# Weight-splitting steps dealt out singly between output pairs, and the softmax numerators normalised on GpSimd, in a fused attention and ELU-MLP kernel

## Chip, cores and metric

One core of one Trainium2 chip runs the whole program. The time is device microseconds of an execution; before the change the median of three runs is 647.06 us (645.84 to 647.61).

## What is computed

Four batches of 12 heads, 448 tokens, head size 64. Attention with a soft cap on the scores, then a two-layer MLP with an ELU between the layers:

```python
scores = cap * tanh(q @ k.T / sqrt(64) / cap)
attn = softmax(scores)                  # sum + 1e-9
x = (attn @ v)                          # (4, 12, 448, 64) -> (1792, 768)
h = x @ w_in                            # 768 -> 2048
g = where(h > 0, h, exp(min(h, 0)) - 1)
out = g @ w_out                         # 2048 -> 768
```

Inputs and output are float32. Each MLP product is done as three TensorE products of rounded halves (high by high, high by low, low by high).

## The kernel before

**Attention.** Twenty-four pairs of heads are worked in 12 rounds of two pairs. A table of times (`AT`, `END`) is sorted once, and that sorted list is the order of every engine's instructions; each engine then runs its own list in order. In a round TensorE makes scores (`tile0`, `scores`), ScalarE does the tanh and the exponential (`act`), TensorE multiplies with the values (`values`, line 408) and makes the row sums (`sums`). VectorE (DVE) adds exponentials (`add`, line 430), splits q and k into high and low halves (lines 358 and 361), copies numerators and sums out of PSUM (`take`, lines 445 and 448), adds and inverts the denominators (`invert`, lines 460 and 463) and also splits the weights and tokens of the MLP. The denominators go through DMAs on SyncE's queue: sums to `den` (line 453), the reciprocals to DRAM (line 465), and from there spread over the partitions into `rb` (`spread`, line 475), two DMAs for each pair. `normalise` (line 480) multiplies the numerator `num` of a pair by its `rb` and gives the tokens `x`. The numerator has five buffers, `rb` two.

**Weights.** There are 32 weight tiles of 128x768, four for each of the 8 rounds of the MLP: two of `w_in`, then two of `w_out`. A tile is split in five steps by a generator (`Weights.steps`): step 1 three DVE operations (lines 123 to 125), step 2 a scaled copy on ScalarE (line 135), step 3 a DVE operation (line 139) and an integer add on GpSimd (line 142), step 4 the rounded high half `wh` on ScalarE (line 149), step 5 the low half `wl` on DVE (line 153). The first four tiles are split in the attention part. There are six `wh` buffers, so tile k takes over that of tile k-6.

**MLP.** A unit is one round r and one block t of tokens (three blocks of 512 columns, one of 256). `Moe.run` deals the units out, software-pipelined by one: it issues `first` of unit i (two hidden tiles `h` and their ELU, ending in `gh` and `gl`), then `second` of unit i-1 (three output pairs e = 0, 2, 4 in a PSUM ring of three, each drained into `acc`: in round 0 by ScalarE, line 285, later by a DVE add, line 300). The weight steps stand around `second`: half of `WRUN[t]` ahead of it and half behind it, 20 steps a round. Steps and drains share ScalarE and DVE, each in program order.

Of the kernel before, what the change touches and what calls it, by code (L numbers as in the profile page):

```python
# [12 lines left out]
ALU = mybir.AluOpType  # L13
# [19 lines left out]
TINY = 2.0**-15  # L33
BLOCKS = [(t, min(BANK, B * S - t)) for t in range(0, B * S, BANK)]
NB = len(BLOCKS)
WRUN = (6, 6, 4, 4)


def pieces(b):

    out = []
    for t, (t0, n) in enumerate(BLOCKS):
        lo, hi = max(t0, b * S), min(t0 + n, (b + 1) * S)
        if lo < hi:
            out.append((t, lo - t0, lo - b * S, hi - lo))
    return out
# [31 lines left out]
class Weights:  # L78
# [77 lines left out]
    def run(self, n):  # L156

        for _ in range(n):
            if self.now is None:
                self.now = self.steps()  # L160
            if next(self.now, self) is self:
                self.now = None

    def get(self, f, second):
        return self.split[f // FT * 2 * FT + f % FT + FT * second]
# [48 lines left out]
class Moe:  # L214
# [54 lines left out]
            if i:  # L269
                self.elu(r, t, i, h)  # L270

    def second(self, r, t):
        nc = self.nc
        width = BLOCKS[t][1]
        end = (r, t) == (NR - 1, NB - 1)
        for e in range(0, NC, 2):
            if end and e == NC - 2:
                continue
            s = self.ps.tile([P, 2, BANK], F32, name=f"o{r}_{t}_{e}", tag="s", bufs=3)[:, :, :width]
            for k in range(2):  # L280
                self.outputs(s[:, k], r, t, e + k)
            if r == 0:
                o = self.late.tile([P, 2, width], F32, name=f"acc{t}_{e}", tag=f"acc{t}", bufs=NC // 2)
                self.acc[t, e] = o
                nc.scalar.activation(out=o, in_=s, func=AF.Copy)  # L285
            else:
                self.finish(r, t, e, 2, s, self.acc[t, e])
        if end:
            for k in range(2):
                s = self.ps.tile([P, 1, BANK], F32, name=f"last{k}", tag=f"pv{k}", bufs=1)[:, :, :width]  # L290
                self.outputs(s[:, 0], r, t, NC - 2 + k)
                self.finish(r, t, NC - 2 + k, 1, s, self.acc[t, NC - 2][:, k : k + 1])
# [13 lines left out]
    def run(self):  # L306

        units = [(r, t) for r in range(NR) for t in range(NB)]
        for i in range(1, len(units) + 1):
            if i < len(units):  # L310
                behind = ()
                if i + 1 < NB:
                    behind = [(b * PPB + c, i + 1) for c in range(PPB) for b in range(B)
                              if any(k == i + 1 for k, *_ in pieces(b))]
                self.first(*units[i], behind)
            n = WRUN[units[i - 1][1]]
            self.wt.run(n // 2)
            self.second(*units[i - 1])
            self.wt.run(n - n // 2)
            self.wt.ahead()  # L320


class Attention:
# [153 lines left out]

    def normalise(self, p):
        x = self.x.new(p)
        self.nc.vector.tensor_tensor(out=x, in0=self.num.pop(p), in1=self.rec.pop(p), op=ALU.mult)  # L480

    def run(self, weights, moe, raw, rawv):
        self.raw.update(enumerate(raw))
# [231 lines left out]
```

## Time and profile before

| what | value |
|---|---|
| median of the runs shown | 647.06 us |
| the profiled execution, its own time | 648.52 us |
| its span in the trace | 646.7 us |
| TensorE busy, share of the span | 97% |
| DVE, ScalarE, GpSimd busy | 72%, 46%, 9% |
| mean granted clock of TensorE | 0.996 |

Busy shares are of the whole span, which holds two stages: the attention up to about 177 us and the MLP behind it. TensorE's busy time is modelled, with ends of matmuls that overlap the next one, so a full TensorE is read from the starts of its matmuls rather than from the share.

### The profile page before, as it was taken

The page shows a single profiled execution, that of the slowest core. Times are in us where ns is not written, and L with a number is a line of the kernel's source. Part 1 is how long each engine was busy: PE and PEld are TensorE (multiplying, and loading weights), DVE is VectorE, ACT ScalarE, POOL GpSimd, SP SyncE. Part 2 cuts the span into 40 slices and gives each one's busy share as a digit, 9 for nine tenths or more (in the row PEclk, how much of TensorE's full clock was granted, in tenths as well). Part 3 has the DMA queues.
Part 4 walks back from the last instruction along what each step waited for, and adds up shares of the span by engine and source line. Part 5 has one row for each costly group of instructions (what it writes and reads, how often), then busy time and mean ns, then how long its engine had stood idle before and what let it go on. Part 6 is the DMA issues. An engine that isn't in the chain of part 4 may idle for free.

```text
span 646.7 us, 8796 instructions
## 1 busy us (share of the span) xinstructions
PE 629.4 (97%) x3408; PEld 463.0 (72%) x3408; DVE 463.8 (72%) x696; ACT 296.7 (46%) x396; POOL 61.2 (9%) x40
## 2 busy tenths in 40 slices
PE   5999999999999899999999999999999999999997
PEld 3334444334478788888888888888888888888886
DVE  4789999999667744776767577666857766776454
ACT  6999999999916544222231322223132322222110
POOL 0010100101001111121111111011111111211000
PEclk9999999999999999999999999999999999999999
DMA  4445565544123111121111111121111111200224
GB/s 162 140 141 186 158 185 148 168 125 132 32 77 126 51 49 50 49 98 31 68 50 50 49 50 55 43 76 71 50 50 50 50 50 49 70 30 0 98 97 152
DMA packets 30065, 54.38 MB, mean 84 GB/s; under 512 B 13377, under 2 KB 17473, under 8 KB 30017
## 3 DMA queue, kind: packets, MB, share of 16 engines
q1 hardware_dynamic: 30016, 53.75, 25.7%
q8 instruction: 29, 0.48, 0.3%
q14 instruction: 20, 0.16, 0.1%
HBM read 47.97 MB, written 5.59 MB: 83 GB/s over the span
## 4 chain that ended last, share of the span: by engine, by line
PE 78%; DVE 13%; DMA 3%; ACT 2%; issue 2%; POOL 1%; SPq 1%; DVEq 0%; POOLq 0%; ACTq 0%
PE o L226 11%; PE o L227 11%; PE o L228 11%; PE h L226 11%; PE h L227 11%; PE h L228 11%; PE pv L408 6%; PE s L366 4%; DVE u L430 3%; DVE xl L211 2%; PE sum L439 2%; DVE qkl L361 1%; DVE num L445 1%; PE s L383 1%; DMA den<-sums 1%
## 5 line engine op out<-in xcount | busy, mean ns | idle before, releaser
L226 PE MATMUL o<-gh,wh 128*128 128x512 f32 (+1 forms) x380 | 138.8, 365 | 2.7 <-ACT acc L285 2.7
L227 PE MATMUL o<-gl,wh 128*128 128x512 f32 (+1 forms) x380 | 138.9, 365 | 0.0
L228 PE MATMUL o<-gh,wl 128*128 128x512 f32 (+1 forms) x380 | 138.7, 365 | 0.0
L227 PE MATMUL h<-xl,wh 128*128 128x512 f32 x288 | 112.2, 390 | 0.3 <-DVE xl L211 0.3
L226 PE MATMUL h<-xh,wh 128*128 128x512 f32 x288 | 112.4, 390 | 0.0
L228 PE MATMUL h<-xh,wl 128*128 128x512 f32 x288 | 112.1, 389 | 0.0
L300 DVE TENSOR_TENSOR acc<-o,acc 128x1024 f32<-128x1024 f32 (+1 forms) x83 | 88.6, 1091 | 31.8 <-PE o L228 31.8
L240 ACT ACTIVATE e<-h 128x512 f32<-128x512 f32 (+1 forms) x64 | 34.7, 542 | 138.8 <-PE h L228 138.8
L401 ACT ACTIVATE p<-s,cap 128x896 f32<-128x896 f32 x84 | 84.7, 1008 | 2.7
L399 ACT ACTIVATE s<-s,tsc 128x896 f32<-128x896 f32 x84 | 81.9, 975 | 5.3 <-PE s L383 2.8
L226 PEld LDWEIGHTS o<-gh,wh 128*128 128x128 f32 x380 | 72.1, 190 | 14.5 <-ACT acc L285 2.9
L408 PE MATMUL pv<-p,vf 128*64 128x448 f32 x368 | 79.3, 552 | 3.0 <-DVE num L445 3.0
L228 PEld LDWEIGHTS o<-gh,wl 128*128 128x128 f32 x380 | 72.1, 190 | 11.4
L227 PEld LDWEIGHTS o<-gl,wh 128*128 128x128 f32 x380 | 72.0, 190 | 11.4
L249 ACT ACTIVATE gh<-e 128x512 fp32r<-128x512 f32 (+1 forms) x64 | 37.0, 578 | 90.2 <-DVE e L244 90.2
L250 DVE TENSOR_TENSOR gl<-e,gh 128x512 fp32r<-128x512 f32 (+1 forms) x64 | 40.0, 626 | 41.2 <-ACT gh L249 41.2
L142 POOL TENSOR_TENSOR pre<-pre,wq 128x768 int32<-128x768 int32 x18 | 34.7, 1929 | 339.7 <-DVE pre L139 339.7
L241 DVE TENSOR_SCALAR e<-e 128x512 f32<-128x512 f32 (+1 forms) x64 | 25.0, 391 | 56.5 <-ACT e L240 56.5
L226 PEld LDWEIGHTS h<-xh,wh 128*128 128x128 f32 x288 | 54.1, 188 | 12.4 <-DVE e L244 0.7
L227 PEld LDWEIGHTS h<-xl,wh 128*128 128x128 f32 x288 | 54.1, 188 | 11.6 <-DVE xl L211 0.7
L228 PEld LDWEIGHTS h<-xh,wl 128*128 128x128 f32 x288 | 54.1, 188 | 11.3
L408 PEld LDWEIGHTS pv<-p,vf 128*64 128x64 f32 x368 | 22.3, 136 | 44.1 <-issue 31.6
(78 smaller groups left out, 770.6 us busy)
## 6 DMA issues: line engine op xcount, KB each, us to landing
pre<-in_w_dram SPq DMA_DIRECT2D x18, 768.0 KB, 4.2
wr<-in_w_dram SPq DMA_DIRECT2D x14, 768.0 KB, 4.2
raw<-in_qk_dram SPq DMA_DIRECT2D x22, 448.0 KB, 4.5
vf<-in_v_dram SPq DMA_DIRECT2D x23, 256.0 KB, 4.1
rb<-rec SPq DMA_DIRECT2D x48, 112.0 KB, 2.9
out_dram<-acc SPq DMA_DIRECT2D x9, 512.0 KB, 2.7
den<-sums SPq DMA_DIRECT2D x96, 1.8 KB, 2.3
pre<-in_qk_dram SPq DMA_DIRECT2D x2, 256.0 KB, 4.1
```

Of the source, the lines that this page charges most:

```text
L142: nc.gpsimd.tensor_tensor(out=vi, in0=vi, in1=q, op=ALU.add)
L226: mm(acc, wh[:, m, :], ph, start=first, stop=False)
L227: mm(acc, wh[:, m, :], pl, start=False, stop=False)
L228: mm(acc, wl[:, m, :], ph, start=False, stop=last)
L240: nc.scalar.activation(out=ev, in_=h, func=AF.Exp)
L249: nc.scalar.activation(out=gh, in_=ev, func=AF.Copy)
L250: nc.vector.tensor_tensor(out=gl, in0=ev, in1=gh.bitcast(F32), op=ALU.subtract)
L300: self.nc.vector.tensor_tensor(out=o, in0=s, in1=o, op=ALU.add)
L366: yield lambda a=a, b=b, i=i: self.nc.tensor.matmul(s, a[o, k], b[o, :S], start=i == 0, stop=i == 2)
L399: self.nc.scalar.activation(out=s, in_=s, func=AF.Tanh, scale=self.con.tsc[:, 0:1])
L401: self.nc.scalar.activation(out=pt, in_=s, func=AF.Exp, scale=self.con.cap[:, 0:1])
L408: self.nc.tensor.matmul(out[o, :S], w[j], x[j], **flags)
```

## The change

```diff
-WRUN = (6, 6, 4, 4)
+WRUN = ((2, 2, 1, 1), (2, 2, 1, 1), (2, 1, 1, 1), (1, 1, 1, 1))
...
-    def second(self, r, t):
+    def second(self, r, t, steps=()):
...
                 self.finish(r, t, e, 2, s, self.acc[t, e])
+            self.wt.run(steps[e // 2])
...
-            n = WRUN[units[i - 1][1]]
-            self.wt.run(n // 2)
-            self.second(*units[i - 1])
-            self.wt.run(n - n // 2)
+            steps = WRUN[units[i - 1][1]]
+            self.wt.run(steps[0])
+            self.second(*units[i - 1], steps[1:])
             self.wt.ahead()
...
     def normalise(self, p):
         x = self.x.new(p)
-        self.nc.vector.tensor_tensor(out=x, in0=self.num.pop(p), in1=self.rec.pop(p), op=ALU.mult)
+        self.nc.gpsimd.tensor_tensor(out=x, in0=self.num.pop(p), in1=self.rec.pop(p), op=ALU.mult)
```

The first number of a tuple is the count of steps ahead of `second`, the other three stand behind the drain of each output pair. A round now has 6 + 6 + 5 + 4 = 21 steps where it had 20.

Three places show what this does to the order.

On GpSimd in the attention, ahead of the weight add of tile 1 and of tile 2 (`x` are the tokens of a pair, `wq` the copy of step 2 that the weight add reads):

```order
 L142 TENSOR_TENSOR pre_81<-pre_81,wq1_671 128x768
+L480 TENSOR_TENSOR x4_871<-num4_514,rb4_763 128x448
+L480 TENSOR_TENSOR x5_873<-num5_581,rb5_768 128x448
+L480 TENSOR_TENSOR x6_1027<-num6_667,rb6_917 128x448
+L480 TENSOR_TENSOR x7_1029<-num7_735,rb7_922 128x448
+L480 TENSOR_TENSOR x8_1185<-num8_821,rb8_1075 128x448
+L480 TENSOR_TENSOR x9_1187<-num9_887,rb9_1080 128x448
 L142 TENSOR_TENSOR pre_81<-pre_81,wq2_1120 128x768
```

The 24 multiplications have left DVE's list for GpSimd's, where they stand between the few weight adds and wait for nothing but their `rb` and what is ahead of them there.

On ScalarE in the MLP, behind the ELU of unit (0, 2), where output unit (0, 1) is drained:

```order
 L135 ACTIVATE wq5_2225<-wr5_2076 128x768
-L149 ACTIVATE wh5_2305<-wv5_2224 128x768
-L285 ACTIVATE acc1_0_2321<-o0_1_0_2308 128x1024
-L285 ACTIVATE acc1_2_2336<-o0_1_2_2323 128x1024
-L285 ACTIVATE acc1_4_2351<-o0_1_4_2338 128x1024
-L135 ACTIVATE wq6_2354<-pre_81 128x768
+L285 ACTIVATE acc1_0_2318<-o0_1_0_2305 128x1024
+L149 ACTIVATE wh5_2320<-wv5_2224 128x768
+L285 ACTIVATE acc1_2_2337<-o0_1_2_2324 128x1024
+L285 ACTIVATE acc1_4_2356<-o0_1_4_2343 128x1024
+L135 ACTIVATE wq6_2339<-pre_81 128x768
```

The drain of the first output pair now stands ahead of `wh5`, which waits for the weight add on GpSimd.

On DVE in round 6, behind the ELU of unit (6, 2), as it is now (before the change `wl30` stood one unit later, behind all drains of unit (6, 2)):

```order
L139 SCALAR_TENSOR_TENSOR pre_81<-pre_81 128x768
L301 TENSOR_TENSOR acc1_0_2318<-o6_1_0_4946,acc1_0_2318 128x1024
L153 TENSOR_TENSOR wl30_4944<-pre_81,wh30_4943 128x768
L123 SCALAR_TENSOR_TENSOR wv31_4961<-wr31_4885 128x768
L124 TENSOR_SCALAR wv31_4961<-wv31_4961 128x768
L125 TENSOR_SCALAR wv31_4961<-wv31_4961 128x768
L301 TENSOR_TENSOR acc1_2_2337<-o6_1_2_4966,acc1_2_2337 128x1024
L301 TENSOR_TENSOR acc1_4_2356<-o6_1_4_4981,acc1_4_2356 128x1024
```

With one step more in each round the splitting has come six steps ahead by round 6: the step that needs the buffer of the round's first weight tile stands ahead of the last unit that reads that tile, and two drains stand behind it.

## Rows read from the trace of the kernel before

**Rows 1.** Chain that ended last: start us, us, work; one round apart.
```profile
45.47 0.91 PE s L383 x8
...
59.01 0.91 PE s L383 x8
```

**Rows 2.** Busy time by stretch, us (instructions), then granted clock, DMA share, GB/s.
```profile
60.00:80.00 20.00, 20.00 (x138) 7.90 (x132) 19.52 (x30) 19.59 (x22) 2.60 (x1) 1.00 0.52 157
...
120.00:140.00 20.00, 19.22 (x134) 8.28 (x134) 19.83 (x37) 19.09 (x20) 0.00 (x0) 1.00 0.49 135
...
226.00:228.00 2.00, 2.00 (x6) 1.57 (x5) 0.94 (x3) 1.18 (x3) 0.00 (x0) 0.50 0.00 0
```

**Rows 3.** Timeline of DVE, attention: start us, us, engine, line, operation, [idle before].
```profile
104.67 0.23 DVE L460 SCALAR_TENSOR_TENSOR den<-den,eps 64x28 f32<-64x28 f32 x1
...
134.39 1.08 DVE L480 TENSOR_TENSOR x<-num,rb 128x448 f32<-128x448 f32 x2
...
148.30 0.23 DVE L460 SCALAR_TENSOR_TENSOR den<-den,eps 64x28 f32<-64x28 f32 x1
```

**Rows 4.** Timeline of GpSimd, the weight add of tile 1.
```profile
74.20 2.60 POOL L142 TENSOR_TENSOR pre<-pre,wq 128x768 int32<-128x768 int32 x1 [26.62 <-DVE pre L139]
```

**Rows 5.** Timeline of DVE beside that add.
```profile
74.04 1.09 DVE L430 TENSOR_TENSOR u<-p,p 128x896 f32<-128x896 f32 x1
75.04 0.62 DVE L448 COPY sums<-sum 128x448 f32<-128x448 f32 x1
75.58 2.18 DVE L430 TENSOR_TENSOR u<-u,p 128x896 f32<-128x896 f32 x1
```

**Rows 6.** Groups by line and shape, count | busy us, mean ns | idle before, releaser.
```profile
L142 POOL TENSOR_TENSOR wv<-wv,wq 128x768 int32<-128x768 int32 x14 | 25.8, 1846 | 188.0 <-DVE wv L139 188.0
...
L124 DVE TENSOR_SCALAR wv<-wv 128x768 f32<-128x768 f32 x14 | 7.8, 561 | 0.5
...
L300 DVE TENSOR_TENSOR acc<-o,acc 128x1024 f32<-128x1024 f32 x63 | 75.9, 1221 | 30.8 <-PE o L228 30.8
```

**Rows 7.** Timeline of SyncE's queue: the DMAs that spread reciprocals, last two rounds.
```profile
177.68 2.37 SPq L475 DMA_DIRECT2D rb<-rec  x4
...
189.04 2.37 SPq L475 DMA_DIRECT2D rb<-rec  x4
```

**Rows 8.** Timeline of DVE from the end of the attention.
```profile
181.23 4.10 DVE L211 TENSOR_TENSOR xl<-x,xh 128x384 fp32r<-128x384 f32 x12
...
192.49 0.62 DVE L480 TENSOR_TENSOR x<-num,rb 128x448 f32<-128x448 f32 x1 [3.18 <-DMA rb<-rec]
...
219.31 0.95 DVE L139 SCALAR_TENSOR_TENSOR wv<-wr,wv 128x768 int32<-128x768 int32 x1
```

**Rows 9.** Timeline of TensorE, 184 to 247 us.
```profile
184.38 0.50 PE L227 MATMUL h<-xl,wh 128*128 128x512 f32 x1 [0.27 <-DVE xl L211]
...
221.12 0.28 PE L228 MATMUL h<-xb,wl 128*128 128x256 f32 x1
...
224.14 0.50 PE L226 MATMUL o<-gh,wh 128*128 128x512 f32 x1 [2.75 <-ACT acc L285]
...
225.19 0.63 PE L227 MATMUL o<-gl,wh 128*128 128x512 f32 x1
...
228.59 0.39 PE L226 MATMUL o<-gh,wh 128*128 128x512 f32 x1
228.82 0.40 PE L227 MATMUL o<-gl,wh 128*128 128x512 f32 x1
...
234.04 0.39 PE L226 MATMUL h<-xh,wh 128*128 128x512 f32 x1
...
242.20 0.28 PE L226 MATMUL o<-gh,wh 128*128 128x256 f32 x1
...
246.52 0.40 PE L226 MATMUL h<-xh,wh 128*128 128x512 f32 x1
```

**Rows 10.** Timeline of ScalarE at the end of round 0's second unit.
```profile
222.33 0.84 ACT L149 ACTIVATE wh<-wv 128x768 fp32r<-128x768 f32 x1 [2.86 <-POOL wv L142]
223.08 2.83 ACT L285 ACTIVATE acc<-o 128x1024 f32<-128x1024 f32 x3
```

## The prediction, made before the changed kernel ran

> **What bounds the kernel now.** I read first the starts of TensorE's matmuls, then the chain that ended last, then the busy time by stretch, then each engine's timeline where two engines meet.
>
> In the MLP TensorE runs matmul behind matmul: 0.23 us from the start at 228.59 to that at 228.82 [rows 9], a wide half unit in 8.16 us (234.04 to 242.20), a narrow one in 4.32 us (242.20 to 246.52). No other engine's work counts there unless TensorE stops. It stops once: between 221.12 and 224.14 us, 2.75 us of it waiting for a drain on ScalarE [rows 9]. That drain stood behind `wh5`, which had waited 2.86 us for the weight add on GpSimd [rows 10], which had waited for the DVE operation at 219.31 [rows 8]. After the stop the granted clock is 0.50 from 226 to 228 us [rows 2], the 1.2 GHz level: the eight matmuls from 225.19 to 228.59 take 0.425 us each [rows 9] instead of 0.23, which is 1.6 us. The stop costs 2.75 + 1.6 = 4.3 us.
>
> In the attention the bound changes hands. Around 50 us the chain runs through TensorE, a round in 59.01 - 45.47 = 13.54 us [rows 1]. From about 90 to 148 us it runs through DVE: the inversions at 104.67 and 148.30 are three rounds apart [rows 3], 14.54 us each, and DVE is busy 19.83 of 20 us [rows 2]. Here a DVE microsecond is a program microsecond. Earlier, from 60 to 80 us, DVE has 0.48 us of slack in 20 [rows 2].
>
> **The normalising.** Two multiplications leave DVE in each round, 1.08 us together [rows 3]. If that were all, the four rounds bound by DVE would fall to TensorE's 13.54 us: -1.0 us each, -4.0 us.
>
> GpSimd's price is bounded by its nearest row, the weight add: 1.85 us for 768 columns [rows 6]. In proportion, 448 columns take 1.08 us; I take that as an estimate. GpSimd itself has time for it; the question is DVE. Two groups show the two engines shutting each other out [rows 4, 5]. The add was released at 74.20, while DVE ran an addition with two SBUF operands; it took 2.60 us, 0.75 longer than alone, so it began to work at about 74.95, when that addition had read its operands. DVE's next addition was dispatched at 75.58 and took 2.18 us instead of 1.09: it stood until the add was done at 76.80. The copy from PSUM at 75.04 ran beside the add at its usual length. So a multiplication on GpSimd stops DVE for up to 1.08 us, unless DVE just then copies from PSUM (four copies of about 0.54 us a round, lines 445 and 448).
>
> The Trainium skill says the same: SBUF — State Buffer, section "Who interferes with whom", has a DVE instruction with two SBUF inputs contend with a GpSimd instruction that reads SBUF, and the trace agrees (2.18 against 1.09 us).
>
> When does GpSimd start? In the last round the spreading DMAs are issued from 189.04 [rows 7] and DVE's wait for the first `rb` ends at 192.49 [rows 8]: 3.45 us behind the first issue, and the second pair's some 1.2 us later, by the spacing of the four issues. That is about six microseconds before DVE used to multiply, in the dense part of its round. What a multiplication costs DVE lies between 0 (inside copies), 0.54 (it starts with a copy and the next operation waits for the rest) and 1.08. The one handover in the rows came with a copy next in line, which speaks for the lower part; but GpSimd got in at 74.95, ahead of DVE's next start at 75.04, which speaks for the upper. I take 0.6. Ten multiplications (x8 to x17) fall into the dense stretch: 10 x (0.6 - 0.54) = **+0.6 us**, bounds -4.0 and 10 x (1.08 - 0.54) = +5.4. The others meet slack and are entered at nothing; without it each pair would cost up to 1.1 us.
>
> Behind them: a numerator copy now also waits for the multiplication five pairs earlier, which is done a round before; x10 stands behind the weight add of tile 2 on GpSimd and x14 behind that of tile 3, which only makes `x` later, and `x` is read rounds later.
>
> **The end of the attention.** x20 and x21 become ready at 177.68 + 3.45 = 181.1 and 182.3 us [rows 7]; DVE starts twelve `xl` subtractions, two SBUF operands each, at 181.23 [rows 8], and TensorE is already waiting 0.27 us for the seventh at 184.38 [rows 9]. The first multiplication stops them about 0.95 us; the second 1.08 or, if DVE goes on, nothing. **+1.4 us**, bounds 0 and +2.0. In return DVE drops the multiplications x20 to x23 and the 3.18 us wait in front of x22 [rows 8]. That work is the beginning of the lateness that ends in the stop at 221 us, so DVE comes there earlier relative to TensorE even after the two stops by x22 and x23.
>
> **Dealing the steps singly.** In round 0 ScalarE's drain of the first pair of unit (0, 1) comes ahead of `wh5`. With the old times it would start at about 219.5, behind `wq5`, and end a microsecond later, before TensorE asks at 221.4; the second pair's drain, behind `wh5`, would end at 224.2 for a TensorE that asks at 224.1. So the stop goes even without an earlier DVE: **-4.3 us**, bounds -4.5 and 0. The same swap at `wh4`, one unit earlier, delays a drain for which TensorE asks about three microseconds later.
>
> In the other rounds TensorE does not stop, so there is nothing to gain. There is something to lose: 21 steps a round. In round 6 `wh30` needs the buffer of tile 24, which is read until half of the narrow `first` is done. Counting from the start of the wide `first` of unit (6, 2): 8.16 + 8.16 + 2.16 = 18.5, then about 0.3 to be seen, 0.85 for `wh30`, 0.95 for `wl30`, as for line 139 [rows 8], 0.95 + 2 x 0.56 for lines 123 to 125, the 0.56 being line 124's [rows 6], and 1.22 for the drain [rows 6]: 23.9. TensorE asks for that tile at 16.32 + 4.32 + 2.72 = 23.4. **+0.5 us**, bounds 0 and 2.1 (with the lower clock behind it). In round 5 only `wl26` is in front, and the drain is done at 21.8: in time.
>
> **Sum.** +0.6 + 1.4 - 4.3 + 0.5 = -1.8 us. Against the profiled execution, 648.52 us, that is 646.7; its time is 1.46 us above the median of the runs, so for the median I say 647.06 - 1.8 = **645.3 us**.
>
> **Rivals.**
> 1. *GpSimd slips between DVE's operations for nearly nothing.* For it: the copy beside the add was not slowed [rows 5]. Against it: 2.18 us. Then -4.0 + 0 - 4.3 + 0.5 = -7.8: 639.3 us. Chance 0.15.
> 2. *Every multiplication stops DVE in full* (slower than before). Place: DVE between 90 and 158 us. +5.4 + 2.0 - 4.3 + 0.5 = +3.6: 650.7 us, and more if the early pairs' slack is used up. It decides from about 0.77 us a multiplication, where the sum is zero. For it: GpSimd's start ahead of DVE's next one. Against: four copies a round. Chance 0.25. The Trainium skill speaks for this one: the same section of SBUF — State Buffer says that casts and scalar operations in a two-port mode also take the shared pair, and "Whoever issues first gets the shared pair for the whole instruction"; no row of before has such an operation beside GpSimd.
> 3. *The stop stays*, because DVE, stopped by x20 to x23, brings ScalarE just as late: +0.6 + 1.4 + 0.5 = +2.5: 649.6 us. Against it: the order itself. Chance 0.07.
> 4. *Running ahead costs several rounds a stop with the lower clock behind it*: three times 2.1 us in place of 0.5: +4.0: 651.1 us. Chance 0.08.
>
> **How the numbers follow.** The forecast has 0.45. Its own range is 643 to 647.5, from 0.45 to 0.8 us a multiplication. The range of 641.0 to 650.8 takes in the forecast, most of rival 2 and rival 3, and part of rival 1. About 0.3% (1.9 us) is what a measurement of this kernel can tell from no change. The forecast sits next to it: of its 0.45 I give 0.24 to faster and 0.21 to the same. With rival 1 faster has 0.39. Rivals 2 to 4 give 0.27 to slower and 0.13 to the same, which makes 0.34.
>
> **What would show it.** Right: the multiplications on GpSimd take 1.0 to 1.2 us alone and more beside DVE's additions; DVE operations of about twice their length appear beside them; the rounds from 104 to 148 us stay at 14.3 to 14.9 us; TensorE has no wait for a drain near 221 us and its clock stays at 1.00 there; it waits some 1.5 us for `xl` near 185. Wrong: rounds near 13.5 (rival 1) or above 15.3 (rival 2), a stop at 221 (rival 3), stops behind the narrow units of rounds 4 to 6 (rival 4).

## The result, and the profile after

The changed kernel takes 653.24 us (median of four runs, 653.04 to 654.7) beside 647.16 us for the kernel before in the same comparison (645.84 to 647.61): 1.0102 times as long, interval 1.0081 to 1.0123. It is slower by 1%; 645.3 us had been forecast, and 653.24 lies above the range.

The profiled execution took 653.3 us, its span 651.4 us, 4.7 us more than before; the granted clock is 0.995. The kernel before was profiled in an execution of 648.52 us, 1.4 us above its median, so the medians lie 6.1 us apart and the spans 4.7; the account below is that of the profiled executions. The page's first part shows who gained work:

```profile
PE 630.1 (97%) x3408; PEld 462.8 (71%) x3408; DVE 468.7 (72%) x672; ACT 295.3 (45%) x396; POOL 95.7 (15%) x64
```

DVE gave away 24 multiplications, 13.3 us of its busy time, and is no less busy for it: 468.7 us beside 463.8. Nineteen of its operations between 47 and 191 us have become longer, by 15.3 us in all. What TensorE waited for, from 30 us on, first before, then after (who <- for whom: us in total, times, longest):

```profile
PE pv L408 <- DVE num L445: 3.0, 7, 0.7
PE o L226 <- ACT acc L285: 2.7, 1, 2.7
PE h L227 <- DVE xl L211: 0.3, 1, 0.3
```

```profile
PE pv L408 <- DVE num L445: 4.9, 4, 2.3
PE sum L439 <- DVE den L460: 3.5, 4, 1.1
PE h L227 <- DVE xl L211: 2.2, 1, 2.2
PE o L226 <- DVE acc L301: 0.2, 1, 0.2
```

The wait for the drain is gone. The waits for DVE in the attention have grown from 3.0 to 8.4 us, with a new kind among them, the row sums behind the inversion. Where the time came from is read off the starts of the inversions on DVE (line 460; [rows 3] has two of before), here three more of before, then five of after:

```profile
36.50 0.23 DVE L460 SCALAR_TENSOR_TENSOR den<-den,eps 64x28 f32<-64x28 f32 x1
...
90.12 0.23 DVE L460 SCALAR_TENSOR_TENSOR den<-den,eps 64x28 f32<-64x28 f32 x1
...
161.59 0.24 DVE L460 SCALAR_TENSOR_TENSOR den<-den,eps 64x28 f32<-64x28 f32 x1
```

```profile
35.95 0.23 DVE L460 SCALAR_TENSOR_TENSOR den<-den,eps 64x28 f32<-64x28 f32 x1
...
92.48 0.23 DVE L460 SCALAR_TENSOR_TENSOR den<-den,eps 64x28 f32<-64x28 f32 x1
...
107.06 0.23 DVE L460 SCALAR_TENSOR_TENSOR den<-den,eps 64x28 f32<-64x28 f32 x1
...
150.96 1.11 DVE L460 SCALAR_TENSOR_TENSOR den<-den,eps 64x28 f32<-64x28 f32 x1
...
166.66 0.23 DVE L460 SCALAR_TENSOR_TENSOR den<-den,eps 64x28 f32<-64x28 f32 x1
```

and from TensorE's timeline, the first hidden matmul of before, then four places of after:

```profile
172.64 0.50 PE L226 MATMUL h<-xh,wh 128*128 128x512 f32 x1
```

```profile
163.39 1.97 PE L408 MATMUL pv<-p,vf 128*64 128x448 f32 x6 [2.32 <-DVE num L445]
...
179.28 0.50 PE L226 MATMUL h<-xh,wh 128*128 128x512 f32 x1
...
192.88 0.50 PE L227 MATMUL h<-xl,wh 128*128 128x512 f32 x1 [2.16 <-DVE xl L211]
...
578.13 0.39 PE L228 MATMUL o<-gh,wl 128*128 128x512 f32 x1
578.76 0.47 PE L226 MATMUL o<-gh,wh 128*128 128x512 f32 x1 [0.24 <-DVE acc L301]
```

| stretch | before, us | after, us | difference |
|---|---|---|---|
| start to the inversion near 36 | 36.50 | 35.95 | -0.55 |
| to the inversion at 90.12 / 92.48 (DVE multiplied x0 to x5, GpSimd x0 to x7) | 53.62 | 56.53 | +2.91 |
| to that at 161.59 / 166.66 (DVE x6 to x15, GpSimd x8 to x17) | 71.47 | 74.18 | +2.71 |
| to the first hidden matmul (DVE x16 and x17, GpSimd x18 and x19, and the clock fall) | 11.05 | 12.62 | +1.57 |
| wait for `xl` | 0.27 | 2.16 | +1.89 |
| stop for the drain at 221 and the slow matmuls behind it | 4.35 | 0 | -4.35 |
| round 6: 0.63 from start to start instead of 0.23 | 0 | 0.40 | +0.40 |
| sum | | | +4.6 |

The sum leaves 0.1 us of the 4.7. The two columns of pairs differ because DVE multiplied a pair just behind an inversion (134.39 in [rows 3]), and GpSimd multiplies it some microseconds ahead of that inversion. The two long stretches, first before, then after (busy PE, PEld, DVE, ACT, POOL, then granted clock, DMA share, GB/s):

```profile
36.50:90.12 53.62, 53.62 (x366) 21.97 (x364) 50.04 (x75) 52.63 (x57) 4.42 (x2) 1.00 0.52 152
90.12:161.59 71.47, 69.17 (x472) 28.68 (x470) 69.02 (x116) 68.01 (x72) 4.44 (x2) 1.00 0.51 151
```

```profile
35.95:92.48 56.53, 55.09 (x376) 22.78 (x374) 52.82 (x68) 53.97 (x58) 15.88 (x10) 1.00 0.50 148
92.48:166.66 74.18, 67.86 (x452) 27.45 (x450) 71.42 (x105) 65.88 (x69) 19.38 (x12) 0.98 0.49 143
```

In the first, DVE is busy 2.8 us longer, 50.04 to 52.82, and idles 3.7 us instead of 3.6: none of its slack was used up. In the second it is busy 2.4 us longer and idles 0.3 us longer. The work of shorter stretches, in the windows of [rows 2] and around the new clock fall (busy PE, PEld, DVE, ACT, POOL, then granted clock, DMA share, GB/s):

```profile
60.00:80.00 20.00, 19.27 (x132) 7.81 (x128) 19.41 (x25) 18.82 (x21) 7.36 (x5) 1.00 0.47 136
...
164.00:166.00 2.00, 2.00 (x6) 0.24 (x2) 2.00 (x4) 0.00 (x0) 0.00 (x0) 0.50 0.00 0
166.00:168.00 2.00, 2.00 (x14) 1.57 (x12) 1.95 (x6) 0.43 (x1) 0.00 (x0) 0.65 0.04 2
...
226.00:228.00 2.00, 2.00 (x19) 2.00 (x19) 1.23 (x2) 1.36 (x2) 0.46 (x1) 1.00 0.00 0
```

From 60 to 80 us, where TensorE was the bound, it is down from 20.00 to 19.27 us while GpSimd is up from 2.60 to 7.36. Behind the stop of 2.32 us at 161 the clock goes to 0.50, the 1.2 GHz level; behind the drains at 226 us it is now 1.00.

Now the two engines side by side. GpSimd's multiplications (a pair behind a weight add, two pairs alone, and one that had DVE idle beside it):

```profile
117.86 2.57 POOL L480 TENSOR_TENSOR x<-num,rb 128x448 f32<-128x448 f32 x2
131.02 3.13 POOL L480 TENSOR_TENSOR x<-num,rb 128x448 f32<-128x448 f32 x2 [10.59 <-DMA rb<-rec]
...
159.12 3.28 POOL L480 TENSOR_TENSOR x<-num,rb 128x448 f32<-128x448 f32 x2 [5.97 <-DMA rb<-rec]
...
200.62 1.15 POOL L480 TENSOR_TENSOR x<-num,rb 128x448 f32<-128x448 f32 x1 [8.87 <-DMA rb<-rec]
```

and DVE in the same microseconds:

```profile
117.94 1.48 DVE L151 CAST wh<-pre 128x768 fp32r<-128x768 f32 x1 [1.40 <-POOL pre L142]
119.34 2.04 DVE L430 TENSOR_TENSOR u<-p,p 128x896 f32<-128x896 f32 x1
...
131.79 1.36 DVE L123 SCALAR_TENSOR_TENSOR pre<-pre 128x768 f32<-128x768 f32 x1
133.19 1.38 DVE L124 TENSOR_SCALAR pre<-pre 128x768 f32<-128x768 f32 x1
...
161.33 1.48 DVE L151 CAST wh<-pre 128x768 fp32r<-128x768 f32 x1
...
187.84 6.00 DVE L211 TENSOR_TENSOR xl<-x,xh 128x384 fp32r<-128x384 f32 x12
```

The two engines take turns: a multiplication lets a DVE operation stand until it is done. The cast of line 151 (the rounded high half of a weight tile, which DVE makes itself in the attention), with one input, took 1.48 us where the group of before shows 557 ns:

```profile
L151 DVE CAST wh<-pre 128x768 fp32r<-128x768 f32 x4 | 2.2, 557 | 2.8 <-POOL pre L142 2.8
```

Line 124, a scalar operation, took 1.38 instead of 0.56, and the addition 2.04 instead of 1.09 [rows 5]. The Trainium skill, SBUF — State Buffer, section "Who interferes with whom", had named casts and scalar operations beside those with two SBUF inputs; the trace agrees now, 1.48 against 0.56 us. The copies of lines 445 and 448 are an exception: 613 and 616 ns on average, 618 before, and 0.61 to 0.62 us for the four that ran beside a multiplication (80.31, 87.34, 103.12 and 131.25 us). The reciprocal of line 463 is another: 0.32 us at 79.98 and 152.11, beside a multiplication, as elsewhere.

ScalarE's order at the place of [rows 10] is the one that the prediction counted on, the first drain ahead of `wh5`:

```profile
226.35 1.01 ACT L285 ACTIVATE acc<-o 128x1024 f32<-128x1024 f32 x1
229.42 0.85 ACT L149 ACTIVATE wh<-wv 128x768 fp32r<-128x768 f32 x1 [2.06 <-POOL wv L142]
230.17 1.92 ACT L285 ACTIVATE acc<-o 128x1024 f32<-128x1024 f32 x2
```

### The profile page after: what moved, and what is told of

The parts are those of the page before. It is cut to its first block, busy times and chain, and to the rows that moved or that the text cites. A ratio compares the mean times of both kernels' runs of the same rounds, so it can differ in the third digit from the quotient of the medians.

```text
span 651.4 us, 8825 instructions
## 1 busy us (share of the span) xinstructions
PE 630.1 (97%) x3408; PEld 462.8 (71%) x3408; DVE 468.7 (72%) x672; ACT 295.3 (45%) x396; POOL 95.7 (15%) x64
## 4 chain that ended last, share of the span: by engine, by line
PE 78%; issue 9%; DVE 8%; DMA 2%; POOL 1%; ACT 0%; SPq 0%; DVEq 0%; POOLq 0%; ACTq 0%
PE o L226 12%; PE o L228 12%; PE o L227 12%; PE h L227 12%; PE h L226 11%; PE h L228 11%; PE pv L408 4%; PE s L366 3%; DVE u L430 3%; PE sum L439 1%; DVE qkl L361 1%; DVE num L445 1%; DMA den<-sums 1%; DMA rec<-den 1%; POOL pre L142 1%
## 5 line engine op out<-in xcount | busy, mean ns | idle before, releaser
L250 DVE TENSOR_TENSOR gl<-e,gh 128x512 fp32r<-128x512 f32 (+1 forms) x64 | 41.6, 650 | 41.3 <-ACT gh L249 41.3
L241 DVE TENSOR_SCALAR e<-e 128x512 f32<-128x512 f32 (+1 forms) x64 | 27.5, 430 | 51.1 <-ACT e L240 51.1
```

Source lines behind the costliest of these rows:

```text
L241: nc.vector.tensor_scalar(out=ev, in0=ev, scalar1=1.0, scalar2=-1.0, op0=ALU.min, op1=ALU.add)
L250: nc.vector.tensor_tensor(out=gl, in0=ev, in1=gh.bitcast(F32), op=ALU.subtract)
```

## The experiments

The theory (A) was that GpSimd's reading of SBUF shuts DVE out, that all of the loss lies in the attention and at the `xl` subtractions, and that the dealing gains its part by itself. The rivals were that the attention waits for the later results instead, that the stop at 221 us goes for another reason than the order, and that running ahead costs more than it showed.

**Each part alone.** First the dealing with DVE's multiplications (against the changed kernel):

```diff
-        self.nc.gpsimd.tensor_tensor(out=x, in0=self.num.pop(p), in1=self.rec.pop(p), op=ALU.mult)
+        self.nc.vector.tensor_tensor(out=x, in0=self.num.pop(p), in1=self.rec.pop(p), op=ALU.mult)
```

> Only the dealing of the steps (21 a round); the multiplications stay on DVE. Theory A (the loss lies in the attention, where each multiplication on GpSimd shuts DVE out; the dealing by itself gains): the attention takes its old length, the stop at 221 us goes (-4.3 us), one short wait for a drain near round 6 stays (+0.4 us): about 643.2 us, 0.6% faster than before. Rival B (running ahead or the new order also costs, for instance by weight adds that now fall beside the ELU's DVE operations): 645 us or more.

Measured: 644.49 us beside 647.86, ratio 0.995 (0.9933 to 0.9967). No stop for a drain, the clock 1.00 throughout from 216 to 234 us, and the 0.24 us wait for `acc` in round 6. That is 1.3 us above the expectation of theory A and below rival B's 645. The dealing is a gain of half a per cent; the change as a whole lost it and nearly twice as much again.

Then the kernel before with GpSimd's multiplications alone:

```diff
-        self.nc.vector.tensor_tensor(out=x, in0=self.num.pop(p), in1=self.rec.pop(p), op=ALU.mult)
+        self.nc.gpsimd.tensor_tensor(out=x, in0=self.num.pop(p), in1=self.rec.pop(p), op=ALU.mult)
```

> Only the multiplications on GpSimd; steps dealt as before the change. Theory A: attention later by 6.6 us and the wait for xl longer by 1.9 us, as in the changed kernel; the stop for the drain stays, since its place in ScalarE's list is the old one, though shorter where DVE is ahead there (1 to 2.75 us, with or without the clock's fall): 653 to 656 us. Rival C (the stop had gone because DVE came earlier, not because of the order): no stop, about 652.5 us.

Measured: 654.81 us, ratio 1.0126 (1.0094 to 1.0158). The wait for `xl` is 2.16 us here too. In the profiled execution, of 653.45 us, TensorE has no wait for a drain, though the old order stands. So there either part removes the stop, and the two parts' gains do not add up. Why it goes here (DVE without x22 and x23 in its list, TensorE itself later) was not tried by itself, and whether it goes in every execution isn't shown: the six spread from 652.77 to 659.39 us, and one was profiled. This run prices the fall of the clock in the attention. TensorE's stop of 2.32 us, up to 163.72 us here, is the one of the changed kernel, but the clock stays at 1.00 behind it:

```profile
164.00:166.00 2.00, 2.00 (x14) 0.88 (x12) 2.00 (x4) 0.00 (x0) 0.00 (x0) 1.00 0.00 0
```

and from the inversion at 166.99 to the first hidden matmul at 178.02 is 11.03 us, as before the change (11.05) and not 12.62. The three profiled executions whose clock falls at this place take 12.56 to 12.69 us for the stretch, the other nine 11.02 to 11.06. So the 1.57 us of the table are the slower clock.

**Contention without moving anything.** GpSimd multiplies `rb` by itself into a buffer that nobody reads, 24 extra products, while DVE keeps its own (against the kernel before):

```diff
+        r = self.rec.pop(p)
+        idle = self.sb.tile([P, S], F32, name=f"idle{p}", tag="idle", bufs=1)
+        self.nc.gpsimd.tensor_tensor(out=idle, in0=r, in1=r, op=ALU.mult)
-        self.nc.vector.tensor_tensor(out=x, in0=self.num.pop(p), in1=self.rec.pop(p), op=ALU.mult)
+        self.nc.vector.tensor_tensor(out=x, in0=self.num.pop(p), in1=r, op=ALU.mult)
```

> The kernel before, with 24 further multiplications on GpSimd (rb by rb into a buffer that nobody reads), released as those of the change are; DVE keeps its own, so nothing waits for GpSimd's result. Theory A (GpSimd's reading shuts DVE out): DVE operations beside them lengthen by 0.6 to 0.8 us each, and with nothing saved on DVE the attention grows by more than in the changed kernel: 8 to 18 us, so 655 to 665 us. Rival D (the loss comes from what waits for the result, x or the numerator's buffer): unchanged, 647 us.

Measured: 662.72 us, ratio 1.0227 (1.0204 to 1.0251). DVE's timeline at the pair behind the weight add of tile 2:

```profile
122.11 1.27 DVE L151 CAST wh<-pre 128x768 fp32r<-128x768 f32 x1 [1.40 <-POOL pre L142]
123.31 1.82 DVE L430 TENSOR_TENSOR u<-p,p 128x896 f32<-128x896 f32 x1
```

Nobody waits for these products, and DVE's operations stand all the same. (One reads a single tile and takes 0.93 us at its shortest, which goes with 1.27 and 1.82 rather than 1.48 and 2.04.) So contention alone is enough for a loss, with no late `x`. The stop for the drain, which the old order has, is 3.3 us here.

**Twenty steps.** The dealing with DVE's multiplications, and one step less for the third block:

```diff
-WRUN = ((2, 2, 1, 1), (2, 2, 1, 1), (2, 1, 1, 1), (1, 1, 1, 1))
+WRUN = ((2, 2, 1, 1), (2, 2, 1, 1), (1, 1, 1, 1), (1, 1, 1, 1))
```

> As e1_deal, but 20 steps a round, so that the splitting doesn't run ahead. Theory A: the short wait in round 6 is absent; about 642.8 us, 0.4 us or less below e1_deal. Rival B: clearly below e1_deal, by 2 us or more.

Measured: 643.44 us, ratio 0.9944 (0.9924 to 0.9964), span 641.5 us against 642.2 with 21 steps. The MLP has no wait left for a drain; 0.4 us of the 0.7 is round 6's. This kernel is called the base below; the runs that follow have other runs of the kernel before beside them (647.58 and 647.71 us in place of 647.86), so a few tenths of a microsecond between medians say nothing.

**The end of the attention alone.** On that base only x20 to x23 on GpSimd:

```diff
+        eng = self.nc.gpsimd if p >= 20 else self.nc.vector
```

> Steps dealt singly at 20 a round, only x20 to x23 on GpSimd. Theory A: relieving DVE there gains nothing, since TensorE doesn't stop in the MLP any more, and x20 and x21 delay the xl subtractions by about 1.9 us: about 645.3 us against 643.4 of e3_deal20. Rival E: DVE's earlier start pays, 643.4 us or less.

Measured: 645.31 us, ratio 0.997 (0.9955 to 0.9984): 1.9 us more than the base, with a wait of 2.16 us for `xl`. With only the last two pairs (`p >= 22`), which have no subtraction beside them:

> Steps dealt singly at 20 a round, only x22 and x23 on GpSimd, whose rb come when the xl subtractions are done. Theory A: TensorE neither waits for them nor gains: 643.4 us as e3_deal20, within 0.5 us. Rival E: below 642.5 us.

Measured: 643.32 us, ratio 0.9939 (0.9919 to 0.9959), the base's time. GpSimd's multiplication is free where DVE has nothing to do (it idles 3.5 us there), and taking a 3.2 us wait out of DVE's list makes no difference once the dealing has removed the stop.

**Taking one place out of the changed kernel.** x20 to x23 back on DVE:

```diff
+        eng = self.nc.gpsimd if p < 20 else self.nc.vector
```

> The changed kernel with the last four multiplications (x20 to x23) back on DVE. Theory A: x20 and x21 no longer stop the xl subtractions, TensorE's wait of 2.16 us near 190 us goes back to about 0.3, and the stop for the drain stays away because of the order of ScalarE's list: 1.9 us faster than the changed kernel, about 651.3 us. Rival E (the stop was away because GpSimd had taken these four and their wait off DVE): a stop of 2 us or more comes back near 230 us, 653 us or more.

Measured: 652.05 us, ratio 1.0068 (1.0045 to 1.0091). The wait for `xl` is 0.3 us again, and 0.31 us of the old wait for the drain is back at 231 us: with these four on DVE again, the new order takes away nine tenths of the stop of 2.75 us. By the medians it is 1.2 us faster than the changed kernel, of 1.9 expected; the intervals of the two overlap. x16 and x17 back on DVE, because TensorE's longest stop in the attention stood behind them:

```diff
+        eng = self.nc.gpsimd if p not in (16, 17) else self.nc.vector
```

> The changed kernel with one pair of multiplications (x16, x17) back on DVE. Theory A: beside these two a q-and-k subtraction took 1.96 us and a cast 1.48 us (1.0 and 0.56 alone), and TensorE stood 2.3 us behind them at 161 us, with the granted clock at 0.50 after it in that one execution. With them gone the stop shrinks to about 0.4 us as before the change: 1 to 2 us faster than the changed kernel, and up to 1.7 us more where the clock doesn't fall. Rival (the loss is spread evenly over the multiplications, 8.5 us over 24 of them): 0.7 us faster.

Measured: 650.83 us, ratio 1.0054 (1.0035 to 1.0073), 2.4 us faster than the changed kernel by the medians. The cast of line 151 takes 0.55 us again and the stop at 161 us shrinks from 2.32 to 0.44 us. In the profiled execution another stop, behind x8 and x9, was 2.05 us where the changed kernel's was 1.24, and the clock fell there, to 0.50 from 106 to 108 us. That isn't the edit's doing: x8 and x9 are multiplied some 55 us ahead of x16, and the order up to there is the same. Executions differ that far; here DVE also waited 0.73 us for a DMA at 95.5 us. A stall taken away at one place leaves the others.

**Early and dense pairs apart.** On the base, x0 to x7 alone, then x8 to x17 alone, on GpSimd:

```diff
+        eng = self.nc.gpsimd if p < 8 else self.nc.vector
```

> The kernel of 20 steps a round with the multiplications on DVE (643.4 us), but x0 to x7 on GpSimd. The prediction entered these eight pairs at nothing, because DVE has slack before 90 us: then 643.4 us, and DVE's inversion near 90 us starts where it did before the change (90.1). Theory A (GpSimd's reading shuts DVE out just ahead of additions for which TensorE waits, and the slack lies elsewhere): the inversion near 90 us starts 2.3 to 2.9 us later, as in the changed kernel, and since DVE has no slack behind it, the lateness stays to the end: 645.7 to 646.5 us. Rival E (the lateness is taken up again in the dense rounds): late at 90 us, but 643.4 to 644.5 us.

Measured: 645.68 us, ratio 0.9968 (0.9956 to 0.9981), 2.2 us above the base. TensorE waits for the row sums, and the inversion of 89.48 us in the base comes here at

```profile
92.87 0.23 DVE L460 SCALAR_TENSOR_TENSOR den<-den,eps 64x28 f32<-64x28 f32 x1
...
106.12 0.23 DVE L460 SCALAR_TENSOR_TENSOR den<-den,eps 64x28 f32<-64x28 f32 x1
```

3.4 us late, 2.1 us at the next round (104.02 in the base), and 1.8 us at the first hidden matmul. So part is taken up again and more than half stays. Seven DVE operations are longer than in the base, by 6.0 us in all: 0.75 us a multiplication. Less eight multiplications of 0.54 that is 1.7 us, near the 1.8 measured, so here the saving was worth its full price. The lateness is larger at 92 us because DVE's work for x6 and x7 used to stand behind that inversion: the round from it takes 13.25 us here and 14.54 in the base.

```diff
+        eng = self.nc.gpsimd if 8 <= p < 18 else self.nc.vector
```

> The same with x8 to x17 on GpSimd and the others on DVE. At the prediction's 0.6 us a multiplication: 10 x (0.6 - 0.54) = 0.6 us, 644.0 us. At the 0.78 us that the lengthened DVE operations of the changed kernel give: 10 x (0.78 - 0.54) = 2.4 us, 645.8 us. If TensorE's clock also falls behind one of its stops, as it did in the changed kernel at 164 us, 1.7 us more: 647.5 us. Theory A expects 645.8 to 647.5 us and TensorE stops of over 1 us for the numerators' copies; the first four inversions of two pairs each as before the change.

Measured: 650.84 us, ratio 1.0049 (1.0027 to 1.007), 7.4 us above the base: more than any of the expectations, and the run that tells most. Ten DVE operations are longer by 8.3 us in all, 0.83 us a multiplication where the changed kernel has 0.77. From the inversion at 89.71 to that at 166.06 is 76.35 us, in the base from 89.48 to 160.94 71.46: 4.9 us lost.

```profile
89.71:166.06 76.35, 69.12 (x466) 28.76 (x464) 73.05 (x108) 67.08 (x71) 19.43 (x12) 0.99 0.47 141
```

DVE is busy 73.05 us of it, in the base 69.01: 4.0 us of the loss is work, and 0.85 us is idling that the base hasn't. The work is 8.3 us of stalls less 4.3 us for eight multiplications. Eight and not ten, because DVE multiplied x16 and x17 behind the inversion that ends the stretch. There their 1.1 us bought nothing: from that inversion to the first hidden matmul is 11.02 us in the base, which has them on DVE, and 11.03 in the run with only GpSimd's multiplications, which has not. Of the 5.4 us of the ten multiplications, then, some 3.5 arrived. The idling comes behind the round of x8 and x9; DVE there, here and (second fence) in the base:

```profile
98.66 1.89 DVE L123 SCALAR_TENSOR_TENSOR pre<-pre 128x768 f32<-128x768 f32 x1
...
100.59 1.38 DVE L124 TENSOR_SCALAR pre<-pre 128x768 f32<-128x768 f32 x1
...
106.01 0.25 DVE L460 SCALAR_TENSOR_TENSOR den<-den,eps 64x28 f32<-64x28 f32 x1
...
106.54 0.55 DVE L211 TENSOR_TENSOR xl<-x,xh 128x448 fp32r<-128x448 f32 x1
108.06 0.62 DVE L445 COPY num<-pv 128x448 f32<-128x448 f32 x1 [0.97 <-PE pv L408]
```

```profile
104.02 0.24 DVE L460 SCALAR_TENSOR_TENSOR den<-den,eps 64x28 f32<-64x28 f32 x1
...
104.75 1.16 DVE L480 TENSOR_TENSOR x<-num,rb 128x448 f32<-128x448 f32 x2
...
106.36 0.62 DVE L445 COPY num<-pv 128x448 f32<-128x448 f32 x1
```

The two stalls, 0.94 and 0.82 us, stand ahead of the numerator copy for which TensorE waits:

```profile
103.15 1.72 PE L408 MATMUL pv<-p,vf 128*64 128x448 f32 x8 [2.11 <-DVE num L445]
```

TensorE then brings the next numerator late, and DVE, which in the base multiplied just there (104.75, 1.16 us), idles 0.97 us for it. The round up to 106.01 is 16.30 us instead of 14.54: the two stalls in full, 1.76 us, with nothing taken off, since its multiplications, x6 and x7, stay on DVE in this run. Three rounds on, from 137.00 to 150.35 us, no operation stands for a multiplication, and the round takes 13.35 us instead of 14.41: there a pair's 1.1 us arrives in full. Behind a stop of 2.32 us in this run's last dense round the clock falls (0.54 from 164 to 166 us), and the stretch up to the first hidden matmul takes 1.5 us more than in the base.

The costs of the places do not simply add: 2.2 (early), 7.4 (dense) and 1.9 (end) are 11.5 us, and the changed kernel is 8.75 us above the dealing alone. In it the dense rounds lose 2.7 us where they lost 4.9 by themselves: x6 and x7 have left DVE there too (1.1 us), the operations stand 0.6 us less, and DVE idles 0.5 us less.

## Why the prediction was wrong, point by point

- **"The others meet slack and are entered at nothing."** This is the step that failed and cost most. x0 to x7 stopped DVE for 5.7 us (0.71 us each), and ahead of the inversion near 90 us only x0 to x5 had been DVE's to save, 3.2 us. The slack was not there to take it: DVE idled 3.6 us in that stretch before and 3.7 after. The changed kernel is 2.9 us later at 92 us, and x0 to x7 alone cost 2.2 us. The 0.48 us in 20 [rows 2] were read rightly, but they are less than one multiplication's stall, and nothing in the rows put a stall where DVE idles.
- **0.6 us for each multiplication.** Too low: 0.77 in the dense rounds of the changed kernel, 1.7 us more for ten. The price was chosen between bounds, near the lower part; the rows of before didn't decide it. The length estimated at 1.08 us is 1.15.
- **The 0.54 taken off for each of ten.** Right in the changed kernel, in part by luck. Ten multiplications did leave DVE between 92.48 and 166.66 us, but x6 to x15 and not x8 to x17; 7.7 us of stalls less 5.4, and 0.3 us of idling, is 2.6 us, and 2.7 was measured. The run of the dense pairs, where x6 and x7 stay, shows that it need not arrive in full: 3.5 of 5.4.
- **The bound.** Right for the dense rounds: the 2.7 us are 2.4 of longer work on DVE and 0.3 of idling. Between the inversion at 161.59 us and the first hidden matmul the 1.1 us of x16 and x17 were worth nothing, as the two stretches of 11.02 and 11.03 us show.
- **No clock fall in the attention** was entered. There is one, behind 2.32 us without matmuls at 161 us, and it makes the stretch in which it lies 1.57 us longer.
- **The attention as a whole:** forecast +0.6, bounds -4.0 and +5.4, measured +6.6 (early 2.9, dense 2.7, clock 1.6, and a start 0.55 earlier, as in the other runs). This is 6.0 of the 6.5 us by which the forecast of -1.8 us missed the span's +4.7. The bounds took only the dense pairs in full and so were not bounds of the whole.
- **The end of the attention:** +1.4 forecast, +1.9 measured: both multiplications (x20, x21) stopped the subtractions, 6.00 us instead of 4.10 [rows 8].
- **The stop at 221 us:** -4.3 forecast, -4.35 measured. The dealing removes it by itself, and so did GpSimd's multiplications in their profiled execution.
- **Running ahead:** +0.5 forecast, +0.4 measured, in the round and at the tile that the prediction named.
- **The rivals.** Rival 2 was right in its mechanism and in the side it ended on; its 650.7 us was too low by the early pairs, which it had only as a remark, and the clock fall. Its test, rounds above 15.3 us between 104 and 148 us, would have missed it: from 107.06 to 150.96 us three rounds take 14.63 us each, which is also inside the 14.3 to 14.9 named as a sign of being right, and the loss lies on either side. Rivals 1, 3 and 4 fell: no multiplication beside dense work was free, the stop did not stay, and there was one wait of 0.24 us in place of several stops.

Of the kernels that ran, the dealing with 20 steps and the multiplications on DVE is the fastest, 643.44 us, with x22 and x23 on GpSimd no different at 643.32; both are about 0.6% faster than the kernel before.

## What to carry to other kernels

Work moved from a nearly full DVE to GpSimd is charged at what it stops on DVE, here 0.71 to 0.83 us for a multiplication that DVE itself did in 0.54, on additions, subtractions, casts and scalar operations alike; copies from PSUM and the small reciprocal went through. Ask for each piece where its stall falls and where its saving does: here the stall came some microseconds ahead of the saving, so that one stretch was charged and the next got the saving. A saving is worth nothing where another engine is the bound, and slack read as an average helps only as far as it is larger than the stalls. Taken apart, a change of two halves may hold a gain: here half a per cent was hidden under a loss of more than one.

## What the runs showed of the hardware that had not been expected

- A GpSimd instruction gets in between two DVE instructions that stand back to back, and two of them stop two DVE instructions in a row: 1.48 and 2.04 us at 117.94 and 119.34 where 0.56 and 1.09 are usual.
- Tiny operations wait as well: the inversion's first step, 64x28, took 1.11 us at 150.96 instead of 0.23.
- Stops of TensorE of nearly the same length do not always bring the clock down. In the changed kernel 2.32 us at 161 did and 2.16 us at 191 did not; with GpSimd's multiplications on the old order the stop of 2.3 us at 161 did not, and 2.16 us at 189 did (0.50 from 194 to 196 us). The one of 2.05 us in the run with x16 and x17 on DVE did, that of 2.11 us in the run of the dense pairs did not. What decides stays open.
